# Reordering the vector engine's sums, the bias path and two interleaved products in a fused attention + MoE kernel

## The chip, the cores and the metric

The kernel runs on one core of a Trainium2 chip. The metric is device time in microseconds (us) of one execution, as the median of several; runs of the same kernel differ by 0.1 to 0.5% in all. A difference below 2% is called "same" by the rule of this study; several differences below are well resolved all the same, because the intervals are about +/-0.15%.

In this text, an eviction is the instruction that reads a finished bank of PSUM (the memory that TensorE writes) out, after which the bank can be used again. Names of engines in the profile: PE is TensorE's matmul, PEld its weight load, DVE is VectorE, ACT is ScalarE, POOL is GpSimd, SP is SyncE.

## The reference

```python
B, H, S, Ns, D = 8, 8, 512, 32, 64        # attention; 8 batches
a  = softmax(x @ state.T / sqrt(D));  xread = a  @ state      # 512 tokens per batch
a2 = softmax(state @ x.T / sqrt(D));  sread = a2 @ x          # 32 state tokens per batch
t  = concat([xread, sread])           # as 4352 tokens x 512
h  = t @ w_in                         # 512 -> 2048
g  = s * relu(h)**2 + b
out = g @ w_out                       # 2048 -> 512
```

## The kernel before

The kernel works in "sweeps", one for each batch, each with 16 slots `f`. In slot `f` of sweep `s`, TensorE computes 128 rows of `h` of batch `s` (the attention weights times `M`, the product of state and `w_in`), ScalarE applies the relu (tile `r`), VectorE squares (`g`, a pair of slots at a time). In the same slots TensorE does the second matmul of batch `s-1` (and at the end of the sweep the first product of batch `s`), a few matmuls per slot, so that both matmuls keep it fed.

For the six middle batches the second matmul is done as seven products of half-size blocks instead of eight (Winograd's form of Strassen's scheme). That needs sums of token blocks (`s`, the function `token_sum`), sums of weight blocks (`wd`, computed once, in sweeps 1 and 2) and sums of products (`qa`, `u`, `qb`), all on VectorE.

```python
def token_sum(b, i, j):                     # VectorE, 128x1024 fp16
    SQ[b, i, j] = spool.tile([P, 4, TH], FP16, name=f"s{i}_{b}_{j}", tag="s")
    o = SQ[b, i, j]
    a11, a21 = G4[b, j][:, :, 0:TH], G4[b, j][:, :, TH:S]
    if i == 3:
        nc.vector.tensor_sub(o, a11, a21)   # the "third operand sum": only needed by product 7
        return
    ...

# the order of the products (p, k from, k to), two matmuls of 256 columns for each k
order = [(1, 0, 8), (6, 0, 4), (2, 0, 4), (6, 4, 8), (2, 4, 8), (7, 0, 8)]
order += [(5, 0, 8), (4, 0, 8), (3, 0, 8)]
bank = {1: "A", 2: "A", 6: "B", 7: "B", 4: "B", 5: "C", 3: "C"}[p]

def done(p):
    if p == 1:   ...scalar_tensor_tensor(q,  acc["A"], s_bc, blk(NH),    ALU.mult, ALU.add)   # qa
    elif p == 6: ...scalar_tensor_tensor(u2, acc["B"], s_bc, kept["qa"], ALU.mult, ALU.add)   # "u", u2
    ...
```

Product 7 goes on accumulating in bank B, where product 6 has just ended. VectorE must read the bank out (`u2`, in the profile `u<-oB,s_bc,qa`) before product 7 may start. Interleaving products 6 and 2 gives VectorE time for it.

The output of batch 0 is computed in the plain form (banks `o`, four of them, through two buffers), and it needs the bias, a sum over the rows of `w_out`, which is computed in sweep 1:

```python
def bias_end():
    ps2 = att_ps([P, DM], FP32, "bias_ps")
    for i in range(2):
        mm(ps2, mean16, wsum[:, i], start=(i == 0), stop=(i == 1))
    nc.vector.tensor_scalar(bias_bc, ps2, b_bc, None, ALU.mult)
    nc.vector.tensor_sub(bias_d, bias_bc[:, 0:NH], bias_bc[:, NH:DM])
    bias_ready.append(True)
    while late:                 # evictions of o_0, o_1 (tile osb) that wait for the bias
        late.pop(0)()

# sweep 1
at(2, bias_sum)
at(3, lambda: att_M(1, 2, "dve"))       # copy of 128x1024 from PSUM, on VectorE
at(4, bias_end)
...
for f in range(NKF):                    # every sweep s
    mm1_x(s, f)
    if s in fast:                       # sweeps 1 to 6
        if f in (5, 9):
            token_sum(s, 3, f // 8)
        if f in (11, 12, 13):
            token_sum(s, (1, 2, 4)[f - 11], 0)
        ...
    if (s == 1 and f in (5, 7, 9, 14)) or (s == 2 and f in (2, 3, 4, 6)):
        with tc.issue_after(G["last"]):     # a "pin": not before the last g
            sums.pop(0)()                   # a weight sum, wd
```

The order of instructions on TensorE is the order of the program. The order on VectorE and ScalarE is chosen by a scheduler when the kernel is built, unless an instruction is pinned behind another with `issue_after`. The pools hold all 8 PSUM banks: two buffers of two banks for attention (`psA`), two of one bank for `h`, two of one bank for `o`, `oA`, `oB` and `oC`. The Trainium skill, "PSUM — Partial Sum Buffer", Specifications (TRN2), gives 8 banks of 512 fp32 values per partition, so nothing is left over and a new output bank can open only after an older one has been evicted.

The softmax here doesn't subtract the row's maximum and nothing guards it: scores larger than these inputs give would overflow.

## Time and profile before

| | before |
|---|---|
| time, median | 223.69 us (first 3 runs: 223.66 to 223.85) |
| span of the profiled execution | 221.8 us |
| PE / DVE / ACT busy | 94% / 67% / 59% |
| granted TensorE clock | 1.00 |
| sweep period (start of u2 to start of the next) | 22.75 us |

TensorE is the engine to fill. Its busy share, however, says little about what is left. The Trainium skill, "Perfetto Trace Analysis", Identifying the Most-Contended Engine, says that matmul busy time is not a good measure of how close a kernel is to its limit, because matmuls are pipelined. The trace agrees: a matmul of 256 columns is recorded with a mean of 273 ns, while seven of them start within 0.76 us, one every 0.109 us. Standing time must be found as a gap between starts: the start of the next instruction minus (start of the last group + its count x 0.109 us). For 512 columns the spacing is 0.217 us. These spacings are those that the Trainium skill, "TensorE: Matmul & The Clock Gate", Back-to-back issue gap, gives by its formula for an isolated matmul at the warm clock (N/2.4 + 2.5 ns; estimates from it: 109 and 216 ns).

The list of waits of the kernel before, TensorE only, shows who held it up. The columns are: engine and tile, what it waited for, us in total, times, longest in us.

```profile
engine line waited for: us in total, times, longest us
PE oB L68 <- DVE u L477: 2.7, 5, 0.8
PE o L68 <- DVE osb L372: 1.7, 1, 1.7
...
PE srT L68 <- DVE sr L293: 0.5, 2, 0.4
...
PE oA L68 <- DVE qa L474: 0.4, 1, 0.4
```

The first line is the product that may not enter bank B before u2 has been read out of it: once in each of five sweeps. The second is the bank for `o_2`, which has to wait until `o_0` has been evicted. (`srT` is a transpose, on TensorE, of `sr`, the attention's result for the state tokens, which VectorE makes.) The timeline of the kernel before, at the first of these in a steady sweep (columns: start us, duration us, engine, line, operation, out<-in, shape, count, and in brackets the idle time before it with its releaser), TensorE first and then VectorE:

```profile
109.90 0.60 PE L68 MATMUL oA<-wo,g 128*128 128x256 f16 x4
110.98 0.49 PE L68 MATMUL oB<-wd,s 128*128 128x256 f16 x3 [0.48 <-DVE u L477]
```

```profile
108.85 0.69 DVE L330 TENSOR_TENSOR g<-r 128x1024 f16<-128x1024 f16 x1 [0.34 <-ACT r L324]
109.58 0.69 DVE L423 TENSOR_TENSOR s<-g 128x1024 f16<-128x1024 f16 x1
110.18 0.74 DVE L477 SCALAR_TENSOR_TENSOR u<-oB,s_bc,qa 128x512 f32<-128x512 f32 x1
```

Four matmuls from 109.90 are issued by 110.34 (4 x 0.109), and product 7 starts at 110.98: TensorE stands still for 0.64 us. The bracket says 0.48 because it counts from the recorded end of the last matmul, which lies 0.16 us after its slot. On VectorE, u2 (L477) stands behind `s` (L423), the third operand sum, which nothing needs until product 7 of this batch, a sweep later. The scheduler has put it there.

The start of `o_2` in sweep 1, again TensorE and VectorE of the kernel before:

```profile
38.12 0.41 PE L68 MATMUL Mps<-wi,stT 64*32 64x512 f16 x8
...
40.19 1.02 PE L68 MATMUL o<-wo,g 128*128 128x512 f16 x4 [1.67 <-DVE osb L372]
```

```profile
35.99 1.22 DVE L268 CAST M<-Mps 128x1024 f16<-128x1024 f32 x1 [0.34 <-PE Mps L68]
37.13 0.68 DVE L330 TENSOR_TENSOR g<-r 128x1024 f16<-128x1024 f16 x1
37.79 0.75 DVE L549 TENSOR_SCALAR bias_bc<-bias_ps,b_bc 128x512 f32<-128x512 f32 x1
38.46 0.68 DVE L423 TENSOR_TENSOR s<-g 128x1024 f16<-128x1024 f16 x1
39.06 0.42 DVE L550 TENSOR_TENSOR bias_d<-bias_bc 128x256 f32<-128x256 f32 x1
39.39 1.40 DVE L372 SCALAR_TENSOR_TENSOR osb<-o,s_bc,bias_bc 128x512 f32<-128x512 f32 x2
```

The eight `Mps` matmuls take 0.34 us, so `o_2` could start at 38.46. It waits for the first `osb`, and ahead of that stand the M copy (1.22 us), the third operand sum and `bias_d`.

### The profile page before, as it was taken

The numbers are of one execution on the slowest core, as the hardware profiler recorded it, in microseconds if no ns is written. First come the engines' busy times: TensorE is split into PE (matmuls) and PEld (weight loads), VectorE is DVE, ScalarE is ACT, GpSimd is POOL, SyncE is SP. The second block draws the span as 40 slices with busy tenths as digits, with TensorE's granted clock in tenths as the row PEclk, the third lists the DMA queues.
The fourth block names the chain that finished last, engine by engine and source line by source line (L and its number), as shares of the span: only waits on it lengthen the run. The fifth ranks groups of instructions, "written<-read, shape, count | busy, mean of one in ns | idle before, by whom it ended". The sixth has DMA issues, their size and how long they took to land.

```text
span 221.8 us, 4633 instructions
## 1 busy us (share of the span) xinstructions
PE 207.4 (94%) x1916; PEld 125.9 (57%) x1916; DVE 147.6 (67%) x262; ACT 131.0 (59%) x223; POOL 41.2 (19%) x72
## 2 busy tenths in 40 slices
PE   7887989799989999999999999999999999999993
PEld 2323333345556675567566765676567677665552
DVE  1686747748997779569956995689568865532221
ACT  3686644579488537965787468756885455323200
POOL 5960010303010310212021201110111111120042
PEclk9999999999999999999999999999999999999999
DMA  6999995999901891981099118111301111121123
GB/s 190 216 205 204 206 179 112 135 208 122 142 0 50 179 193 22 185 139 68 27 157 179 52 49 177 62 47 50 95 32 66 47 50 47 50 95 47 50 47 95
DMA packets 38776, 23.72 MB, mean 107 GB/s; under 512 B 24100, under 2 KB 36644, under 8 KB 38756
## 3 DMA queue, kind: packets, MB, share of 16 engines
q0 software_dynamic: 15792, 16.72, 38.1%
q1 hardware_dynamic: 22548, 6.62, 16.3%
q8 instruction: 15, 0.25, 0.5%
q10 hardware_dynamic: 416, 0.10, 0.2%
q14 instruction: 5, 0.04, 0.1%
HBM read 17.33 MB, written 8.91 MB: 118 GB/s over the span
## 4 chain that ended last, share of the span: by engine, by line
PE 71%; DVE 13%; DMA 8%; ACT 4%; issue 1%; POOL 1%; SPq 0%
PE h L68 18%; PE oB L68 14%; PE o L68 10%; PE oC L68 9%; PE oA L68 6%; DMA xn<-in_x_dram 5%; DVE g L330 4%; PE h_sr L68 3%; PE o_sr L68 3%; PE Mps L68 3%; DMA xf<-in_x_dram 2%; ACT r L324 2%; DVE u L477 2%; PE D L68 1%; DVE osb L372 1%; DVE s L423 1%
## 5 line engine op out<-in xcount | busy, mean ns | idle before, releaser
L324 ACT ACTIVATE r<-h 128x512 f16<-128x512 f32 x126 | 74.4, 599 | 56.6 <-PE h L68 54.9
L68 PE MATMUL h<-a,M 128*128 128x512 f16 x256 | 75.0, 379 | 1.2 <-DVE a L242 0.7
L330 DVE TENSOR_TENSOR g<-r 128x1024 f16<-128x1024 f16 x64 | 44.2, 691 | 24.7 <-ACT r L324 24.5
L68 PEld LDWEIGHTS <-g 128*128 128x128 f16 x432 | 40.8, 98 | 24.8 <-issue 5.8
L68 PEld LDWEIGHTS <-s 128*128 128x128 f16 x384 | 35.7, 98 | 18.3 <-issue 7.5
L466 POOL DMA_DIRECT2D out_dram<-osb x24 | 16.2, 675 | 121.1 <-DVE osb L464 104.0
L68 PE MATMUL o<-wo,g 128*128 128x512 f16 (+1 forms) x144 | 32.3, 356 | 1.7 <-DVE osb L372 1.7
L68 PEld LDWEIGHTS <-M 128*128 128x128 f16 x256 | 24.6, 98 | 10.5 <-issue 2.5
L68 PE MATMUL oB<-wd,s 128*128 128x256 f16 x192 | 27.9, 273 | 2.8 <-DVE u L477 2.7
L68 PE MATMUL oA<-wo,g 128*128 128x256 f16 x192 | 27.8, 273 | 0.4 <-DVE qa L474 0.4
L266 ACT CAST M<-Mps 128x1024 f16<-128x1024 f32 x25 | 25.3, 1010 | 0.6
L68 PE MATMUL Mps<-wi,stT 64*32 64x512 f16 x256 | 13.2, 385 | 1.4 <-DMA wi<-in_moe_w_in_dram 1.4
L68 PE MATMUL oC<-wd,s 128*128 128x256 f16 x96 | 14.3, 273 | 0.0
L68 PEld LDWEIGHTS <-stT 64*32 64x32 f16 x384 | 5.2, 90 | 14.9 <-issue 10.7
L68 PE MATMUL oB<-wd,g 128*128 128x256 f16 x96 | 13.6, 273 | 0.0
L68 PE MATMUL oC<-wo,s 128*128 128x256 f16 x96 | 13.4, 273 | 0.0
L324 ACT ACTIVATE r_sr<-h_sr 128x256 f16<-128x256 f32 x16 | 6.1, 382 | 10.7 <-PE h_sr L68 10.7
L242 DVE TENSOR_TENSOR a<-E,R 128x1024 f16<-128x1024 f16 (+1 forms) x9 | 5.7, 632 | 7.0 <-ACT R L241 7.0
L464 DVE SCALAR_TENSOR_TENSOR osb<-oC,s_bc,u 128x512 f32<-128x512 f32 x12 | 9.0, 748 | 1.4 <-PE oC L68 1.4
L240 ACT ACTIVATE L<-D 128x1024 f32<-128x1024 f32 (+1 forms) x9 | 8.3, 926 | 2.5 <-PE D L68 2.5
L217 ACT ACTIVATE E<-T 128x512 f16<-128x512 f32 x16 | 9.4, 596 | 0.7 <-PE T L68 0.7
L330 DVE TENSOR_TENSOR g_sr<-r_sr 128x512 f16<-128x512 f16 x8 | 3.4, 424 | 9.5 <-ACT r_sr L324 9.5
(80 smaller groups left out, 202.3 us busy)
## 6 DMA issues: line engine op xcount, KB each, us to landing
out_dram<-osb POOLq DMA_DIRECT2D x31, 256.0 KB, 2.5
xn<-in_x_dram POOLq DMA_DIRECT2D x7, 512.0 KB, 9.3
wi<-in_moe_w_in_dram POOLq DMA_DIRECT2D x4, 512.0 KB, 9.0
wo<-in_moe_w_out_dram POOLq DMA_DIRECT2D x4, 512.0 KB, 16.0
xf<-in_x_dram SPq DMA_DIRECT2D x2, 512.0 KB, 4.8
out_dram<-osb_sr POOLq DMA_DIRECT2D x8, 64.0 KB, 2.0
out_dram<-osb SPq DMA_DIRECT2D x2, 128.0 KB
st<-in_state_dram POOLq DMA_DIRECT2D x1, 192.0 KB, 19.6
```

Source lines behind the costliest of these rows:

```text
L68: return nc.tensor.matmul(out, lhsT, rhs, start=start, stop=stop, tile_position=tp, is_transpose=is_transpose, skip_group_check=True,)
L217: nc.scalar.activation(a["E"][:, g, :].rearrange("p (m t) -> p m t", m=2), T[:, :, 256 * i : 256 * i + 256], AF.Exp, scale=scale, accum_ou ...
L240: nc.scalar.activation(a["L"][:, sl], Dps, AF.Ln)
L242: nc.vector.tensor_mul(a["a4"][:, sl], a["E"][:, sl], a["R"][:, sl])
L266: nc.scalar.copy(dst, ps)
L324: nc.scalar.activation(r16[:, f % 2], hps, AF.Relu)
L330: nc.vector.tensor_mul(gt[:, f % 4 - 1 : f % 4 + 1], r16, r16)
L372: nc.vector.scalar_tensor_tensor(osb, ops, s_bc, bias_bc[:, n0:n1], ALU.mult, ALU.add)
L423: nc.vector.tensor_sub(o, a11, a21)
L464: nc.vector.scalar_tensor_tensor(osb, acc[bank], s_bc, add, ALU.mult, ALU.add)
L466: nc.gpsimd.dma_start(dst[j][:, :, n0 : n0 + NH], osb)
L477: nc.vector.scalar_tensor_tensor(u, acc["B"], s_bc, kept["qa"], ALU.mult, ALU.add)
```

## The change

The change takes urgent reads of PSUM out from behind sums that can wait. It has three parts. (1) The third operand sum is emitted two slots later and pinned behind the last `g`. (2) Products 6 and 2 are interleaved 4-3-4-5 instead of 4-4-4-4, so that product 6 ends two matmuls earlier. (3) The bias matmuls move up by one slot, the M copy of the same slot goes to ScalarE, and `bias_d` moves down to slot 9.

```diff
-        order = [(1, 0, 8), (6, 0, 4), (2, 0, 4), (6, 4, 8), (2, 4, 8), (7, 0, 8)]
+        order = [(1, 0, 8), (6, 0, 4), (2, 0, 3), (6, 4, 8), (2, 3, 8), (7, 0, 8)]
...
         nc.vector.tensor_scalar(bias_bc, ps2, b_bc, None, ALU.mult)
-        nc.vector.tensor_sub(bias_d, bias_bc[:, 0:NH], bias_bc[:, NH:DM])
         bias_ready.append(True)
...
+    def bias_half():
+        nc.vector.tensor_sub(bias_d, bias_bc[:, 0:NH], bias_bc[:, NH:DM])
...
-                at(3, lambda: att_M(1, 2, "dve"))
-                at(4, bias_end)
+                at(3, lambda: att_M(1, 2, "act"))
+                at(3, bias_end)
                 at(6, lambda: att_stT(2))
+                at(9, bias_half)
...
-                    if f in (5, 9):
-                        token_sum(s, 3, f // 8)
+                    if f in (7, 11):
+                        with tc.issue_after(G["last"]):
+                            token_sum(s, 3, f // 8)
```

## The prediction

> **What bounds the kernel now.** TensorE. The page has it busy 94% of a 221.8 us span at full granted clock; VectorE is busy 67%, ScalarE 59%. The Trainium skill, "Trainium Kernel Development and Optimization", Performance Expectations, warns that matmul busy time misleads because matmuls are pipelined, so I count issue gaps in the timeline instead: in a run of 256-column matmuls, starts are 0.109 us apart (seven from 81.69 to 82.45), 512-column ones 0.217 us. Only where TensorE stands still is there time to win. The list of waits, TensorE only, has two large lines: bank oB waiting for u2 (2.7 us, 5 times, at most 0.8) and o waiting for osb (1.7 us, once). By issue gaps they cost 1.7 us at 38.46 (once), 0.97 us in sweep 2 (63.79) and 0.64 us in each of sweeps 3 to 6: 5.2 us in all, the ceiling of the gain.
>
> **What the change does.** No arithmetic goes or comes; the instructions are reordered, and one M copy of 128x1024 moves from VectorE (1.22 us) to ScalarE (1.0 us), which idles there.
>
> 1. Bias, sweep 1. Now bias_bc (37.79) follows the M copy and the next g; then the third operand sum (0.60) and bias_d (0.42) run before the output eviction that frees the bank for o_2, which starts at 40.19 and could at 38.46. Afterwards bias_bc should start near 36.9, the eviction near 37.7, and end near 38.4: this wait disappears, about -1.7 us.
> 2. But VectorE's new order puts two token sums (1.2 us) between g and the eviction of o_2, which had 0.7 us of slack before oA opens in its bank: a new wait of about 0.6 us. From about 51 us on VectorE runs without pauses up to u2 at 62.99 (its timeline), and that queue has one 0.6 us sum more, less a 0.12 us pause. So the wait for u2 in sweep 2 is VectorE's backlog and hardly shrinks. Sweeps 1 and 2 together: -1.2 us up to the seventh product.
> 3. Sweeps 3 to 6. The third sum (0.60) no longer stands between g and u2, and the sixth product ends two matmuls (0.22 us) earlier. u2 follows g directly: start 109.45 instead of 110.18, released about 110.25, against a natural start of the seventh product at 110.34. The wait vanishes with some 0.1 us to spare: 4 x -0.64 = -2.6 us.
> 4. Given back. In sweep 2 the transposes srT wait for sr, which now follows one more sum: +0.5 us. In sweep 7 the sixth product's second half starts two matmuls earlier and waits for its sum, which already made it wait 0.2 us: +0.2 us.
>
> All this is on TensorE's own line, so on the critical path: -1.2 - 2.6 + 0.7 = -3.1 us.
>
> **Prediction: 220.6 us, 8 in 10 between 219.5 and 221.8.** Chances: faster by over 2% 0.06, within 2% 0.93, slower by over 2% 0.01.
>
> **What the profile would show.** Right: no wait of o for osb near 38 us; the sweep period (22.75 us between u2 starts at 110.18 and 132.93) becomes about 22.1; oB's waits for u2 fall from 2.7 us to under 1, what remains being in sweep 2; oA waits for osb about 0.6 us near 51 us; srT's waits for sr rise to about 1 us. Wrong: the period stays near 22.75, or oB waits for s (the sum that the sixth product needs) by more than 0.1 us a sweep.
>
> **What would make it wrong.** The slack of 0.1 us in step 3 may not exist; the third sum, moved to slot 11, may push VectorE's end-of-sweep work (output eviction, qa, sums) into the next sweep's first products. If the sweep 2 backlog dissolves, the gain approaches 5 us.

## The result, and the profile after

The changed kernel took 220.5 us (median of 4 runs, 220.33 to 220.71) against 223.77 us of the kernel before on the same chip (4 runs, 223.66 to 224.17). The ratio is 0.9851 with a 95% interval of 0.9834 to 0.9868. Ratios here are the mean time of one kernel's fast runs over that of the other's fast runs of the same rounds, so they are not quite the ratio of the medians quoted. The class is "same" (within 2%), and the gain of 3.3 us is clear of the noise.

| | before | after |
|---|---|---|
| span of the profiled execution | 221.8 us | 218.9 us |
| PE / DVE / ACT busy | 94 / 67 / 59% | 95 / 66 / 60% |
| sweep period | 22.75 us | 22.10 us (u2 at 86.11 and 108.21) |

The list of waits of the changed kernel, TensorE only:

```profile
PE srT L68 <- DVE sr L293: 1.0, 2, 0.8
...
PE oB L68 <- DVE u L477: 0.6, 1, 0.6
...
PE oA L68 <- DVE osb L372: 0.5, 1, 0.5
PE oB L68 <- DVE s L429: 0.4, 2, 0.3
...
```

The wait for u2 is left in one sweep of five; the wait of `o` for `osb` is gone; three others have come or grown (srT, oA for osb, oB for s). The steady sweep of the changed kernel at the same place, TensorE and VectorE:

```profile
108.65 0.60 PE L68 MATMUL oA<-wo,g 128*128 128x256 f16 x4
109.09 0.49 PE L68 MATMUL oB<-wd,s 128*128 128x256 f16 x3
```

```profile
107.60 0.69 DVE L330 TENSOR_TENSOR g<-r 128x1024 f16<-128x1024 f16 x1 [0.34 <-ACT r L324]
108.21 0.75 DVE L477 SCALAR_TENSOR_TENSOR u<-oB,s_bc,qa 128x512 f32<-128x512 f32 x1
```

u2 now follows `g` at once, ends at 108.96, and product 7 starts at 109.09, which is exactly 4 x 0.109 us after 108.65: no gap. In sweep 1, TensorE of the changed kernel:

```profile
38.26 0.41 PE L68 MATMUL Mps<-wi,stT 64*32 64x512 f16 x8
38.61 1.04 PE L68 MATMUL o<-wo,g 128*128 128x512 f16 x4
...
51.17 0.41 PE L68 MATMUL Mps<-wi,stT 64*32 64x512 f16 x8
52.10 0.60 PE L68 MATMUL oA<-wo,g 128*128 128x256 f16 x4 [0.52 <-DVE osb L372]
...
62.70 0.49 PE L68 MATMUL oB<-wd,s 128*128 128x256 f16 x3 [0.58 <-DVE u L477]
```

`o_2` starts without a gap at 38.61 (1.7 us won), but oA, in the buffer of `o_2`, now waits 0.52 us (0.59 us by starts), because the scheduler has put two token sums ahead of the eviction of `o_2`, as VectorE of the changed kernel shows:

```profile
49.49 0.69 DVE L330 TENSOR_TENSOR g<-r 128x1024 f16<-128x1024 f16 x1 [0.32 <-ACT r L324]
50.09 0.69 DVE L423 TENSOR_TENSOR s<-g 128x1024 f16<-128x1024 f16 x1
50.70 0.69 DVE L427 TENSOR_TENSOR s<-g,g 128x1024 f16<-128x1024 f16 x1
51.30 0.75 DVE L372 SCALAR_TENSOR_TENSOR osb<-o,s_bc,bias_bc 128x512 f32<-128x512 f32 x1
```

At product 7 of sweep 2 the kernel is only 1.09 us ahead of the one before (62.70 against 63.79). As predicted, VectorE's queue decides here.

### The profile page after: what moved, and what is told of

Same layout as the page of the kernel before. It is cut to its first block, busy times and chain, and to the rows that moved or that the text cites. A ratio compares the mean times of both kernels' runs of the same rounds, so it can differ in the third digit from the quotient of the medians.

```text
span 218.9 us, 4633 instructions
## 1 busy us (share of the span) xinstructions
PE 207.2 (95%) x1916; PEld 125.9 (58%) x1916; DVE 145.3 (66%) x261; ACT 131.6 (60%) x224; POOL 41.5 (19%) x72
## 4 chain that ended last, share of the span: by engine, by line
PE 73%; DVE 13%; DMA 8%; ACT 2%; POOL 1%; issue 1%; SPq 0%
PE h L68 18%; PE oB L68 14%; PE o L68 11%; PE oC L68 9%; PE oA L68 7%; DMA xn<-in_x_dram 5%; PE Mps L68 4%; PE h_sr L68 3%; PE o_sr L68 3%; DVE g L330 3%; DMA xf<-in_x_dram 3%; DVE s L429 1%; DVE s L427 1%; PE D L68 1%; DVE osb L464 1%; PE V L68 1%
## 5 line engine op out<-in xcount | busy, mean ns | idle before, releaser
L330 DVE TENSOR_TENSOR g<-r 128x1024 f16<-128x1024 f16 x64 | 44.2, 691 | 22.1 <-ACT r L324 21.9
L68 PE MATMUL oA<-wo,g 128*128 128x256 f16 x192 | 27.2, 272 | 0.8 <-DVE osb L372 0.5
L266 ACT CAST M<-Mps 128x1024 f16<-128x1024 f32 x26 | 26.3, 1011 | 0.6
```

Source lines behind the costliest of these rows:

```text
L68: return nc.tensor.matmul(out, lhsT, rhs, start=start, stop=stop, tile_position=tp, is_transpose=is_transpose, skip_group_check=True,)
L266: nc.scalar.copy(dst, ps)
L330: nc.vector.tensor_mul(gt[:, f % 4 - 1 : f % 4 + 1], r16, r16)
```

## The experiments

Ten runs were made: eight new kernels (x1 to x8), and the changed kernel and x4 once more (y1, y2); each with a result equal to the reference within its tolerance and each timed in five rounds beside the kernel before. All those named x1 to x4 ran in one call on one chip (before: 223.62 us), x5 to x8 in a second (before: 223.44 us), y1 and y2 in a third (before: 223.57 us).

The theory: TensorE's standing time is the only thing to win; in steady sweeps it is due to u2's place in VectorE's queue, and in sweeps 1 and 2 to the length of that queue. Two rivals: u2 waits for the end of product 6, so that the interleave makes the difference; or time won in one place is given back in the next.

### x1_bias: the bias part alone

```diff
-                at(3, lambda: att_M(1, 2, "dve"))
-                at(4, bias_end)
+                at(3, lambda: att_M(1, 2, "act"))
+                at(3, bias_end)
+                at(9, bias_half)          # and bias_d out of bias_end, as in the change
```

> The bias part alone on the kernel before. Theory (each part acts where the timeline puts it, TensorE's standing still being the only thing to win): the start of o_2 is no longer held by the M copy and bias_d, but the third operand sum of sweep 1 still runs ahead of the output eviction, so its wait falls from 1.7 us to about 0.5 us; the sweep period stays 22.75 us; no new wait of oA for osb. 222.4 us, 1.2 us under before. Rival (the time won in sweep 1 is given back at VectorE's queue before u2 in sweep 2): 223.5 us or more.

Measured: 222.34 us, 1.28 us under before, ratio 0.9941 (0.9927 to 0.9955). The wait of `o` for `osb` is 0.4 us in the list, no wait of oA for osb appears, and u2 starts at 86.17 and 108.91: the period is 22.74 us. VectorE of x1 in sweep 1 shows what is left:

```profile
36.85 0.74 DVE L549 TENSOR_SCALAR bias_bc<-bias_ps,b_bc 128x512 f32<-128x512 f32 x1
37.52 0.68 DVE L423 TENSOR_TENSOR s<-g 128x1024 f16<-128x1024 f16 x1
38.11 1.40 DVE L372 SCALAR_TENSOR_TENSOR osb<-o,s_bc,bias_bc 128x512 f32<-128x512 f32 x2
```

The third operand sum still stands between the bias and the eviction. What was won is kept to the end of the kernel; nothing is given back. Which of the three edits inside the bias part (the earlier matmuls, the M copy on ScalarE, the later `bias_d`) wins how much was not tested.

### x2_sums: the later, pinned sums alone

```diff
-                    if f in (5, 9):
-                        token_sum(s, 3, f // 8)
+                    if f in (7, 11):
+                        with tc.issue_after(G["last"]):
+                            token_sum(s, 3, f // 8)
```

> The later, pinned sums alone. Theory: in sweeps 3 to 6 the wait of oB for u2 is gone (period about 22.1 us, 2.6 us won); in sweeps 1 and 2 about as much is won at o_2 (0.5 us) as is lost at oA and in VectorE's queue ahead of u2; srT waits 0.5 us more. 221.6 us, 2.1 us under before. Rival (the interleave is needed, since u2 waits for the sixth product's end and not for the queue): period 22.3 us or more, 222.5 us.

Measured: 221.41 us, 2.21 us under before, ratio 0.9899 (0.9883 to 0.9915). The period is 22.10 us (u2 at 87.20 and 109.30), u2 follows `g` by 0.61 us, and oB waits for u2 only once, for 0.8 us. The interleave is not needed for this. The waits of srT for sr come to 1.0 us and that of oA for osb to 0.5 us, as in the full change; `o` still waits 1.2 us for osb, since the M copy and `bias_d` are where they were.

### x3_order: the interleave alone

```diff
-        order = [(1, 0, 8), (6, 0, 4), (2, 0, 4), (6, 4, 8), (2, 4, 8), (7, 0, 8)]
+        order = [(1, 0, 8), (6, 0, 4), (2, 0, 3), (6, 4, 8), (2, 3, 8), (7, 0, 8)]
```

> The 4-3-4-5 interleave alone. Theory: u2 stands behind the third sum in VectorE's queue, so ending the sixth product two matmuls earlier frees nothing: period 22.75 us, oB's waits for u2 as before (2.7 us), and sweep 7 loses 0.2 us at the sixth product's sum. 223.9 us, 0 to 0.3 us over before. Rival (u2 waits for the sixth product's end): 0.2 us won in each of five sweeps, 222.7 us.

Measured: 223.73 us against 223.62, ratio 1.0007 (0.9992 to 1.0022): no gain. TensorE and VectorE of x3 in the same sweep as above:

```profile
108.52 0.28 PE L68 MATMUL oB<-wd,s 128*128 128x256 f16 x1
...
109.72 0.60 PE L68 MATMUL oA<-wo,g 128*128 128x256 f16 x4
110.80 0.49 PE L68 MATMUL oB<-wd,s 128*128 128x256 f16 x3 [0.48 <-DVE u L477]
```

```profile
109.40 0.69 DVE L423 TENSOR_TENSOR s<-g 128x1024 f16<-128x1024 f16 x1
110.01 0.74 DVE L477 SCALAR_TENSOR_TENSOR u<-oB,s_bc,qa 128x512 f32<-128x512 f32 x1
```

Product 6 ends with the one matmul at 108.52 (recorded end 108.80), 1.2 us before u2 begins. u2 is behind `s` in the queue, and the wait is the same 0.48 us as before. The rival that u2 waits for product 6 has fallen for the steady sweeps. In sweep 2 the list shows a wait for u2 of 0.6 us instead of 0.8, but nothing was won there: product 6 now comes two matmuls earlier to a sum that is not ready, and a new wait of oB for `s` appears (0.4 us in two places, this and sweep 7).

The three parts alone give -1.28, -2.21 and +0.11 us, which add up to -3.38 us; together they gave -3.3 us (and -3.1 us in y1 below). The parts hardly interact.

### x4_sums_bias: the change without the interleave

```diff
-        order = [(1, 0, 8), (6, 0, 4), (2, 0, 3), (6, 4, 8), (2, 3, 8), (7, 0, 8)]   # of the changed kernel
+        order = [(1, 0, 8), (6, 0, 4), (2, 0, 4), (6, 4, 8), (2, 4, 8), (7, 0, 8)]   # as before
```

> The changed kernel with the old 4-4-4-4 interleave. Theory: the interleave has no share in the gain, period still about 22.1 us, and sweep 7's wait of oB for its sum is 0.2 us shorter: 220.3 us, 0.2 us under the changed kernel. Rival (the interleave gives the slack of 0.1 us that lets the wait vanish): period 22.2 to 22.3 us and 221 us or more.

Measured: 220.19 us, ratio 0.9846 (0.983 to 0.9862). The period is 22.10 us, and there is no wait for u2 in the steady sweeps. So the slack that the prediction counted on does not come from the interleave either.

### y1_after and y2_x4: the changed kernel and x4 in the same rounds

No edit: y1 is the changed kernel, y2 is x4.

> The changed kernel again, in the same rounds as x4, to tell whether the interleave costs anything in it. Theory (sweep 7's wait for the sixth product's sum is 0.2 us longer with the interleave, and nothing is won elsewhere): 0.2 us slower than x4, 220.4 against 220.2 us. Rival (no effect): equal within 0.05 us.

> x4 again (bias part and pinned sums, old interleave), beside the changed kernel in the same rounds. Theory: 0.2 us faster than the changed kernel, 220.2 us. Rival: equal within 0.05 us.

Measured: y1 220.46 us (220.24 to 220.57), ratio 0.9860 (0.9846 to 0.9873); y2 220.13 us (219.95 to 220.47), ratio 0.9847 (0.9834 to 0.9860). The means differ by 0.13%, about 0.3 us, in the expected direction, but the intervals overlap, so the times alone do not settle 0.2 us. The traces show where it would come from. TensorE in sweep 7 of y1, and then of y2:

```profile
171.13 0.38 PE L68 MATMUL oA<-wo,g 128*128 128x256 f16 x2
171.80 0.61 PE L68 MATMUL oB<-wd,s 128*128 128x256 f16 x4 [0.29 <-DVE s L429]
```

```profile
171.28 0.60 PE L68 MATMUL oA<-wo,g 128*128 128x256 f16 x4
171.95 0.39 PE L68 MATMUL oB<-wd,s 128*128 128x256 f16 x2
```

In y1 the gap before oB is 171.80 - (171.13 + 2 x 0.109) = 0.45 us; in y2 it is 171.95 - (171.28 + 4 x 0.109) = 0.23 us. With the interleave, product 6 comes two matmuls earlier to a sum that is not ready, and waits 0.22 us longer.

### x5_early: the second half of the third sum earlier in sweeps 1 and 2

```diff
-                    if f in (7, 11):
+                    if f in (7, 9 if s < 3 else 11):      # on x4
```

> As x4 (bias part and pinned sums, old interleave), but in sweeps 1 and 2 the second half of the third sum is pinned in slot 9 instead of 11. Theory: VectorE's queue from 49 us to u2 in sweep 2 has one sum (0.6 us) less, oA's wait for osb (0.5 us) goes, and srT's waits for sr fall from 1.0 to about 0.5 us; u2 still waits in sweep 2 (backlog of the weight sums), 0.8 us as before or a little more. 219.2 us, 1.0 us under x4. Rival (the order of the sums in sweeps 1 and 2 only moves the same wait from one place to the next): 220.0 us or more.

Measured: 219.24 us, ratio 0.9813 (0.98 to 0.9827). Against x4 that is 1.0 us less (220.19 against 219.24, with before at 223.62 and 223.44; by the ratios 0.33%, 0.7 us). In the list the wait of oA for osb is gone, srT's waits fell from 1.0 to 0.5 us, and the wait for u2 in sweep 2 stayed at 0.8 us. Moving one operation of 0.6 us out of two crowded stretches was worth 0.7 to 1.0 us, where the two waits that went add up to 1.0 us in the list, and no new wait appears in the list after the start-up.

### x6_wd_early: the weight sums out of the crowded stretch

```diff
-                if (s == 1 and f in (5, 7, 9, 14)) or (s == 2 and f in (2, 3, 4, 6)):
+                if (s == 1 and f in (5, 6, 7, 8, 9, 10)) or (s == 2 and f in (5, 6)):   # on x5
```

> x5 and, in addition, weight sums moved forward out of VectorE's dense stretch: six of the eight in sweep 1 between slots 5 and 10, two in sweep 2. Theory (u2's wait in sweep 2 is the queue's backlog): 1.8 us of work less before u2 in sweep 2, the waits of oB for u2 and of oA for qa vanish, 217.7 us, 1.5 us under x5. Rival (u2 in sweep 2 waits for the sixth product's last sum or for TensorE itself): at most 0.5 us under x5; or VectorE, now fuller in sweep 1, delays g and a new wait appears there.

Measured: 217.70 us, ratio 0.9748 (0.9735 to 0.9761), 1.54 us under x5. VectorE ahead of u2 in sweep 2, of the changed kernel and then of x6:

```profile
59.49 0.69 DVE L414 TENSOR_TENSOR wd<-wo,wo 128x1024 f16<-128x1024 f16 x1
60.09 0.69 DVE L486 TENSOR_TENSOR qb<-qa,bias_d 128x512 f32<-128x512 f32 x1
60.69 0.69 DVE L330 TENSOR_TENSOR g<-r 128x1024 f16<-128x1024 f16 x1
61.29 0.69 DVE L414 TENSOR_TENSOR wd<-wo,wo 128x1024 f16<-128x1024 f16 x1
61.89 0.75 DVE L477 SCALAR_TENSOR_TENSOR u<-oB,s_bc,qa 128x512 f32<-128x512 f32 x1
```

```profile
58.09 0.68 DVE L486 TENSOR_TENSOR qb<-qa,bias_d 128x512 f32<-128x512 f32 x1
58.84 0.69 DVE L330 TENSOR_TENSOR g<-r 128x1024 f16<-128x1024 f16 x1
59.45 0.75 DVE L477 SCALAR_TENSOR_TENSOR u<-oB,s_bc,qa 128x512 f32<-128x512 f32 x1
```

Without the two `wd` in between, u2 follows `g`, and x6's list of waits has neither a wait for u2 nor one for qa. The wait for u2 in sweep 2 was VectorE's backlog.

### x7_srt: two transposes one slot later

```diff
-                at(13, lambda: att_srT(0))
-                at(13, lambda: att_srT(1))
+                at(14, lambda: att_srT(0))      # in sweep 2, on x6
+                at(14, lambda: att_srT(1))
```

> x6 and, in addition, the two extra srT transposes of sweep 2 one slot later (14 instead of 13). Theory: their wait for sr (0.5 us) vanishes: 217.2 us, 0.5 us under x6. Rival: the wait of srT is overlapped by other work or moves to what follows, and nothing is won.

Measured: 216.75 us (216.65 to 216.88), ratio 0.9702 (0.9689 to 0.9715), 0.95 us under x6 where 0.5 was expected. TensorE of x6 at this place:

```profile
73.14 0.59 PE L68 MATMUL h<-a,M 128*128 128x512 f16 x2
74.09 0.23 PE L68 MATMUL srT<-ident,sr 128*128 128x128 f16 x1 [0.35 <-DVE sr L293]
74.47 0.23 PE L68 MATMUL srT<-ident,sr 128*128 128x128 f16 x1 [0.15 <-DVE sr L293]
```

By starts, the first transpose stands 74.09 - (73.14 + 2 x 0.217) = 0.52 us, and the second 0.38 us less its own spacing of 0.055 us (x7 issues two of them in 0.11 us), 0.32 us: 0.84 us together. The brackets add up to 0.50 us because they start at the recorded ends of matmuls. The expectation had taken the figure from the list; the count of starts was the right one. The last 0.1 us is not explained. This version beats both kernels of the case, by 3.0% over the one before.

### x8_pin_only: pinned in the old slots

```diff
-                    if f in (7, 11):
+                    if f in (5, 9):         # on x4: pinned, but in the slots of before
```

> Bias part and sums pinned in their old slots 5 and 9 in every sweep (no move by two slots). Theory: the pin, which puts the sum behind g and so behind u2, is what matters, not the slot: period about 22.1 us and 219.2 us, as x5, 1.0 us under x4. Rival (the later slots matter: in slot 5 the sum delays the a and u3 operations that follow): period over 22.2 us, 220 us or more.

Measured: 219.29 us, ratio 0.9815 (0.9802 to 0.9828), the same as x5, with a period of 22.10 us (u2 at 85.03 and 107.13). So the pin is what wins the steady sweeps, and not the two slots. The two slots even cost something: x4 is the same kernel with the sums two slots later, and x8 is faster by 0.31% by the ratios (0.7 us; 0.9 us by the medians). Its list has no wait of oA for osb, and 0.5 us at srT instead of 1.0. Most of what the change gave back was therefore the price of its own delay of the sums in sweeps 1 and 2. A version with the slots changed and no pin (on x1) was built and not run: its order on every engine is, instruction for instruction, that of x1. Without the pin, the scheduler moves the sum back ahead of u2.

## Why the prediction was right

- **Total.** Predicted 220.6 us (219.5 to 221.8), measured 220.5 us. The predicted gain of 3.1 us compares with 3.3 us, and with 3.1 us in y1.
- **Step 1, the bias.** Predicted: bias_bc near 36.9 and the eviction near 37.7, no wait for `o_2`. Measured: 37.01 and 37.79, no gap at 38.61. x1 showed that the sums contribute to this: without them 0.4 us of the wait stays.
- **Step 2, the new wait and the backlog.** Predicted: oA waits about 0.6 us, the wait for u2 in sweep 2 hardly shrinks, and product 7 of sweep 2 is 1.2 us ahead. Measured: 0.52 us in the list (0.59 by starts) and 0.58 us left at u2 (0.74 by starts, where it was 0.97); the 0.2 us less at u2 is taken up by a new wait of product 6 for its sum in this sweep, which the prediction did not have. Product 7 is 1.09 us ahead; TensorE began this stretch 0.15 us later in that execution (the `h` before the bias sum at 32.76 instead of 32.61), so 1.24 us on the same footing. x5 and x6 removed exactly the operations named and won the time.
- **Step 3, the steady sweeps.** Predicted: a period of about 22.1 us, with u2 directly after `g`. Measured: 22.10 us. The prediction listed two reasons for this, the sum and the interleave. x2 and x3 show that only the first one acts: with the sum behind u2, u2 waits for `g`, and with the sum ahead of it, it waits for the sum. In sweeps 2 to 6 the end of product 6 is never the last; in sweep 7, with the interleave, u2 does wait 0.37 us for it (at 173.75), but TensorE does not wait for u2 there.
- **Step 4, given back.** Predicted: +0.5 us at srT and +0.2 us in sweep 7. The list shows srT's waits going from 0.5 to 1.0 us, and the gap in sweep 7 going from 0.23 (y2, and the kernel before) to 0.45 us (y1). The sign that the prediction named for being wrong, oB waiting for `s` by more than 0.1 us a sweep, shows in sweeps 2 and 7 only.
- **What was wrong.** "5.2 us in all, the ceiling of the gain" and "If the sweep 2 backlog dissolves, the gain approaches 5 us". x6 is 5.7 us and x7 6.7 us under the kernel before. The ceiling counted the two largest waits by starts, but left out the smaller ones (qa, srT) as if they were nothing; counted by starts in the kernel before, srT was 0.84 us (77.54 and 77.92) and qa 0.56 us (58.11), which with the 5.2 us makes 6.6 us, an estimate close to what x7 won.

## What to carry to other kernels

When an engine that is only two thirds busy holds up the one that is full, look at what stands directly ahead of the urgent instruction in its queue; a sum of 0.6 us that nobody waits for cost 0.64 us of TensorE in each sweep, and one pin behind the right instruction removed it. Check the order that the scheduler builds, since moving the code by two slots without the pin changed nothing in the order, and with the pin the two slots cost about 0.7 us. Count standing time by the starts of pipelined instructions and not by their recorded ends, and after each gain look for what the same move pushes into: here the change gave back 0.6 us at oA, 0.5 us at srT and 0.2 us in sweep 7, and x4, x5 and x8 show that none of it was needed.

## What the Trainium skill lacked or had wrong

- "TensorE: Matmul & The Clock Gate", Back-to-back issue gap: the page says that a stream of weight loads and matmuls sustains about 131 ns per matmul of 512 columns and about 81 ns for 128 columns, and that its formula N/2.4 + 2.5 ns holds for an isolated one. In this kernel, where every matmul has its own weight load (1916 of each), the spacing in the stream is 0.217 us for 512 columns and 0.109 us for 256, as the formula has it, and two transposes of 128 columns took 0.11 us (x7, from 74.83 to 74.94). The stream figures do not fit.
- "Perfetto Trace Analysis", Identifying the Most-Contended Engine: weight-load busy time went from 57% to 59% between the kernel before and x7 and does not point to any of the gaps. For TensorE the page lacks the count by starts: the profile's idle time before a matmul is short by about 0.16 us for each gap (recorded 273 ns against a spacing of 109 ns; 379 against 217 ns).
- "VectorE: DVE Perf Modes", The TRN2 errata: the table's 58 + FD/2 cycles for a sum of 128x1024 fp16 (estimate from it: 594 ns) and 120 + FD cycles for a read of 512 fp32 from PSUM (658 ns) fit the spacing in a full queue, 0.60 and 0.66 us. The recorded durations are longer (0.69 and 0.74 us). The page compares its row with recorded durations and finds it short; here the row is the spacing, and a full queue is costed with spacings.
- "VectorE: DVE Perf Modes", The DRAIN you can't avoid: it says that a semaphore between VectorE instructions costs nothing extra. In steady sweeps an instruction that reads what the one directly ahead of it wrote (`s` L423 behind `g`, `s` L429 behind L427) started 0.72 to 0.73 us after it, against 0.60 us for an independent one. The page's measurement was of another case, so this is a gap rather than a contradiction.
